# Gate logits of two batches in one PSUM bank: sharing the turn and the choice of experts

## The chip, the cores and the metric

The kernel runs on one core of one Trainium2 chip. The metric is the device time of one execution in microseconds (us). The kernel before takes 679.64 us, the median of three runs (679.59 to 681.14). The profile comes from one further execution, whose span is 676.8 us; positions in the trace count from its start.

The engines go by these names: PE is TensorE (matrix products), PEld is its loading of weights, DVE is VectorE, ACT is ScalarE, POOL is GpSimd and SP is SyncE, which here issues transfers. A step of the loop is one pass of the attention loop shown below, numbered by its `n`.

## The reference: what is computed

Attention with a local mask in half of the heads and a strided one in the others, followed by a mixture of experts in which a position may keep the expert of the position before it. Cut to what matters:

```python
# attention: batch 8, heads 8, positions 576, head size 64
scores = scale * np.matmul(q, k.transpose(0, 1, 3, 2))
scores = np.where(masks, scores, -1e9)          # local: rel < 32; strided: same residue mod 32
attn = softmax(scores)
x = np.matmul(attn, v)                          # -> x[b, s, 512]
...
# experts: E = 8, hidden size 1024
logits = np.einsum('bsd,de->bse', x, w_gate)    # 8 gate logits of a position
local_gate = sigmoid(x @ w_local)               # one more column
for b in range(B):
    for s in range(S):
        fresh_e = argmax(logits[b, s])
        e = fresh_e if s == 0 or local_gate[b, s] < 0.5 else prev_e
        prev_e = e
        p = softmax(logits[b, s])
        out[b, s] = p[e] * (relu(x[b, s] @ w1[e]) @ w2[e])
```

The nine columns (8 gates and the local gate) are one small matrix of weights, padded to 32 columns. All of it is float32.

## The kernel before: the parts concerned

Attention runs batch by batch, four pairs of heads to a batch. A step `n` of the loop starts the scores of pair `n`, multiplies the values of pair `n - 2` and transposes the result of pair `n - 3`, so that `x` of a batch lies turned (features on partitions) in `xT`. With the fourth pair of batch `b` turned, in step `n = 4b + 7`, the gate logits of that batch are made:

```python
wgs = consts.tile([P, DK, GC], F32, name="wgs")          # GC = 32 columns, 9 of them used
...
sel = consts.tile([P, E + 1], F32, name="sel")           # 1 where row % 32 == column
...
def gates(b):
    xT = st["xT", b]
    gl = rows.tile([P, S], F32, name="gl")
    for a in range(2):                                   # two halves of 288 positions
        s = slice(a * (S // 2), (a + 1) * (S // 2))
        pg = psX.tile([P, 512], F32, name="xps")         # one PSUM bank
        for kk in range(DK):                             # 4 parts of the 512 features
            pe(nc.tensor.matmul, pg[kk * GC:(kk + 1) * GC, 0:S // 2], lhsT=wgs[:, kk, :], rhs=xT[:, kk, s],
               start=True, stop=True)
        nc.scalar.copy(out=gl[:, s], in_=pg[:, 0:S // 2])
    st["gl", b] = gl
```

The four parts of the features land on four groups of 32 rows. Of each group the first nine rows hold something. The next function adds the four groups and turns the logits at once, by a product with `sel` (positions now on partitions, 6 blocks of 96), and chooses:

```python
def choices(b):
    gl = st["gl", b]
    ps = psX.tile([P, 512], F32, name="xps")
    for t in range(LT):                                  # 6 blocks of 96 positions
        pe(nc.tensor.matmul, ps[0:LQ, t * (E + 1):(t + 1) * (E + 1)], lhsT=gl[:, t * LQ:(t + 1) * LQ],
           rhs=sel, start=True, stop=True)
    lt = small.tile([LQ, LT, E + 1], F32, name="lt")
    nc.scalar.copy(out=lt, in_=...)
    nc.vector.tensor_reduce(mx, lg, axis=AX.X, op=Alu.max)
    nc.vector.tensor_tensor(ex, lg, mxb, op=Alu.subtract)
    nc.scalar.activation(ex, ex, Act.Exp)
    yield
    # next step: seven small operations of VectorE (eq, eq, code, code, fr, codes ...)
    nc.vector.tensor_tensor(codes[:, :, b], spread(code, [LQ, LT, E]), spread(fr, [LQ, LT, E]), op=Alu.mult)
    yield
    # the step after it: four more (sum, + 1e-9, reciprocal, product), then the gates are written out
    nc.sync.dma_start(out=xd[b * S:(b + 1) * S, D:DX]..., in_=ex)
    yield
```

The loop, in which the order of each engine's instructions is fixed as it is written:

```python
for n in range(len(pairs) + 6):
    if n < len(pairs):
        ...                                              # loads of a later batch (SyncE)
        for u in pairs[n]:
            scores(u)                                    # PE "sps", then ACT exp -> e
    last = pairs[n - 4][0] if 0 <= n - 4 < len(pairs) else None
    done = last.b if last and last.pair == PAIRS - 1 else None
    if done is not None:
        gates(done)
        ...
    for g in range(2):
        mask_out(pairs[n][g])                            # DVE, e * mask
        values(pairs[n - 2][g])                          # PE "vps", DVE reciprocal and product -> xl, xs
        if g == 0:
            next(chosen, None)
            if done is not None:
                chosen = choices(done)
                next(chosen)
    ...                                                  # store_x: POOL writes xl, xs out to xd
    turn_x(...)                                          # PE transposes "xps", ACT copies -> xT
```

Between these, pieces of `route` are placed: from step 17 on it routes the first three batches (BE = 3), from the `codes` of batches 0 to 2, on TensorE and VectorE; and pieces of the first expert's products fill the end of the stage. After attention `route` runs again for all eight batches beside the first experts.

Of the kernel before, what the change touches and what calls it, by code (L numbers as in the profile page):

```python
# [9 lines left out]
F32 = mybir.dt.float32  # L10
BF16 = mybir.dt.bfloat16
I32 = mybir.dt.int32
# [7 lines left out]
P = 128  # L20
# [63 lines left out]
def spread(ap, shape):  # L84

    dims = list("abcd"[:len(shape) - 1])
    left = " ".join(dims[:-1] + [f"({dims[-1]} o)"])
    right = " ".join(dims + ["o"])
    return ap.rearrange(f"{left} -> {right}", o=1).to_broadcast(shape)


def across(ap, shape):

    return ap.rearrange("a (o b) -> a o b", o=1).to_broadcast(shape)
# [177 lines left out]
def attention(ctx, tc, careful, psX, psS, fill, q, k, vl, vs, wg, xd, cc, codes, inv):  # L272
# [9 lines left out]
    small = ctx.enter_context(tc.tile_pool(name="small", bufs=3))  # L282
    psV = ctx.enter_context(tc.tile_pool(name="psV", bufs=1, space=PSUM))

    wgs = consts.tile([P, DK, GC], F32, name="wgs")


    maskL = consts.tile([LK, LQ], F32, name="maskL")
# [45 lines left out]
    nc.vector.tensor_scalar(ri, ri, GC - 1, None, Alu.bitwise_and)  # L334
    rf = consts.tile([P, 1], F32, name="rf")
    nc.vector.tensor_copy(rf, ri)
    ce = consts.tile([P, E + 1], I32, name="ce")
    nc.gpsimd.iota(ce, pattern=[[1, E + 1]], base=0, channel_multiplier=0)
    sel = consts.tile([P, E + 1], F32, name="sel")
    nc.vector.tensor_copy(sel, ce)  # L340
    nc.vector.tensor_scalar(sel, sel, rf, None, Alu.is_equal)

# [18 lines left out]
    def pe(product, *args, **kw):  # L361

        with tc.issue_after(st["pe"]) if "pe" in st else nullcontext():
            st["pe"] = product(*args, **kw).ins  # L364
# [19 lines left out]
    def load_first():  # L384


        for n in range(2 * PAIRS + 2):
            if n == PAIRS + 2:
                nc.sync.dma_start(out=wgs, in_=wg.rearrange("(k p) e -> p k e", p=P))
            if n < 2 * PAIRS:  # L390
                b, pair = divmod(n, PAIRS)
                grp, i2 = divmod(pair, 2)
                if i2 == 0:
                    places(b, grp)
                qt, kt = st["q", b, grp], st["k", b, grp]
                hq, hk = LT // 2 * LQ, LT // 2 * LQ + STRIDE
                for c, d in (((slice(0, hq), slice(0, hk)), (slice(hq, S), slice(hk, KW))) if n == 0 else
                             ((slice(0, S), slice(0, KW)),)):
                    nc.sync.dma_start(out=qt[:, i2, c], in_=q[b][:, pair, c])
                    (nc.sync if n else nc.scalar).dma_start(out=kt[:, i2, d], in_=k[b][:, pair, d])  # L400
            if n >= 2:
                b, pair = divmod(n - 2, PAIRS)
                grp, i2 = divmod(pair, 2)
                nc.sync.dma_start(out=st["v", b, grp][:, i2], in_=(vs if grp else vl)[b][:, i2])
# [90 lines left out]
    def turn_x(b, pair):  # L495
        grp, i2 = divmod(pair, 2)
        if pair == 0:
            st["xT", b] = rows.tile([P, DK, S], F32, name="xT")
        src = st["x", b, grp]
        o = st["xT", b][:, pair, :]  # L500
        o = (o.rearrange("x (i s p) -> x s i p", s=2, p=LQ // 2) if grp == 0 else
             o.rearrange("x (s p c) -> x s p c", s=2, c=STRIDE))
        for g in range(2):
            u = pairs[b * PAIRS + pair][g]
            r, m = u.rows, u.m
            ps = psX.tile([P, 512], F32, name="xps")
            for i in range(m):
                pe(nc.tensor.transpose, ps[:, i * P:i * P + r], src[0:r, u.t0 + i, i2 * P:(i2 + 1) * P],
                   ident[0:r, 0:r])
            if grp == 0:  # L510
                nc.scalar.copy(out=o[:, :, 3 * g:3 * g + 3].rearrange("x s i p -> x i s p"),
                               in_=ps[:, 0:m * P].rearrange("x (i s p) -> x i s p", i=m, s=2)[:, :, :, 0:LQ // 2])
            else:
                c, n = SBLK[u.t0]
                pt = ps[:, 0:m * P].rearrange("x (i s p) -> x s i p", i=m, s=2)[:, :, :, 0:n * SP // 2]
                for s in range(2):
                    nc.scalar.copy(out=o[:, s, :, c:c + m * n].rearrange("x p (i c) -> x i p c", i=m),
                                   in_=pt[:, s].rearrange("x i (p c) -> x i p c", c=n))

    def gates(b):  # L520

        xT = st["xT", b]
        gl = rows.tile([P, S], F32, name="gl")
        for a in range(2):
            s = slice(a * (S // 2), (a + 1) * (S // 2))
            pg = psX.tile([P, 512], F32, name="xps")
            for kk in range(DK):
                pe(nc.tensor.matmul, pg[kk * GC:(kk + 1) * GC, 0:S // 2], lhsT=wgs[:, kk, :], rhs=xT[:, kk, s],
                   start=True, stop=True)
            nc.scalar.copy(out=gl[:, s], in_=pg[:, 0:S // 2])  # L530
        st["gl", b] = gl

    def filling():
        with tc.issue_after(st["pe"]):
            st["pe"] = next(fill).ins

    def choices(b):

        gl = st["gl", b]
        ps = psX.tile([P, 512], F32, name="xps")  # L540
        for t in range(LT):
            pe(nc.tensor.matmul, ps[0:LQ, t * (E + 1):(t + 1) * (E + 1)], lhsT=gl[:, t * LQ:(t + 1) * LQ],
               rhs=sel, start=True, stop=True)
        lt = small.tile([LQ, LT, E + 1], F32, name="lt")
        nc.scalar.copy(out=lt, in_=ps[0:LQ, 0:LT * (E + 1)].rearrange("p (t e) -> p t e", e=E + 1))
        lg = lt[:, :, 0:E]
        mx = small.tile([LQ, LT], F32, name="gmx")
        nc.vector.tensor_reduce(mx, lg, axis=AX.X, op=Alu.max)
        mxb = spread(mx, [LQ, LT, E])
        ex = small.tile([LQ, LT, E], F32, name="ex")  # L550
        nc.vector.tensor_tensor(ex, lg, mxb, op=Alu.subtract)
        nc.scalar.activation(ex, ex, Act.Exp)
        yield

        eq = small.tile([LQ, LT, E], F32, name="eq")
        nc.vector.tensor_tensor(eq, lg, mxb, op=Alu.is_equal)
        nc.vector.tensor_tensor(eq, eq, across(down, [LQ, LT, E]), op=Alu.mult)
        code = small.tile([LQ, LT], F32, name="code")
        nc.vector.tensor_reduce(code, eq, axis=AX.X, op=Alu.max)
        nc.vector.tensor_tensor(code, pos8, code, op=Alu.subtract)  # L560
        fr = small.tile([LQ, LT], F32, name="fr")
        nc.vector.scalar_tensor_tensor(fr, lt[:, :, E], FRESH, start, Alu.is_le, Alu.max)

        nc.vector.tensor_tensor(codes[:, :, b], spread(code, [LQ, LT, E]), spread(fr, [LQ, LT, E]), op=Alu.mult)
        yield
        sm = small.tile([LQ, LT], F32, name="gsm")
        nc.vector.tensor_reduce(sm, ex, axis=AX.X, op=Alu.add)  # L567
        nc.vector.tensor_scalar(sm, sm, 1e-9, None, Alu.add)
        nc.vector.reciprocal(out=sm, in_=sm)
        nc.vector.tensor_tensor(ex, ex, spread(sm, [LQ, LT, E]), op=Alu.mult)  # L570
        nc.sync.dma_start(out=xd[b * S:(b + 1) * S, D:DX].rearrange("(t p) e -> p t e", p=LQ), in_=ex)
        yield

    pairs = [[Unit(b, pair, g) for g in range(2)] for b in range(B) for pair in range(PAIRS)]
# [7 lines left out]
    for n in range(len(pairs) + 6):  # L582
        if n < len(pairs):
            b, pair = divmod(n, PAIRS)
            if n >= PAIRS and pair % 2 == 0 and b + 1 < B:
                load(b + 1, pair // 2)
            for u in pairs[n]:
                (scores_shifted if careful else scores)(u)

        last = pairs[n - 4][0] if 0 <= n - 4 < len(pairs) else None  # L590
        done = last.b if last and last.pair == PAIRS - 1 else None
        if done is not None:
            gates(done)
            if done == B - 1:
                filling()
        yield n, 0, (st["pe"], st["dve"])
        for g in range(2):
            if n < len(pairs) and not careful:
                mask_out(pairs[n][g])
            if g == 0:  # L600
                yield n, 1, (st["pe"], st["dve"])
            if 0 <= n - 2 < len(pairs):
                values(pairs[n - 2][g])
            if g == 0:
                with tc.issue_after(st["dve"]):
                    next(chosen, None)
                    if done is not None:
                        chosen = choices(done)
                        next(chosen)
                if done == B - 1:  # L610
                    filling()
                yield n, 2, (st["pe"], st["dve"])
        if 0 <= n - 2 < len(pairs):
            u = pairs[n - 2][1]
            if u.i2 == 1:
                store_x(u.b, u.grp)
        if 0 <= n - 3 < len(pairs):
            u = pairs[n - 3][0]
            turn_x(u.b, u.pair)
            if n - 3 >= len(pairs) - 2:  # L620
                filling()
# [702 lines left out]
```

## Time and profile before

| what | value |
|---|---|
| time, median of three | 679.64 us (679.59 to 681.14) |
| span of the profiled execution | 676.8 us |
| first matmul of the scores | 7.66 us |
| last turning of gates starts (batch 7) | 145.15 us |
| gate matmuls, mean | 128, 412 ns |
| turning matmuls, mean | 96, 231 ns |
| copies of gates PSUM to SBUF (ACT) | 16, 399 ns |
| copies of turned logits (ACT) | 8, 200 ns |
| granted TensorE clock | 0.99 |

The busy time of an engine is the sum of its instructions' spans. Matmuls overlap, so the mean of one is longer than the distance to the next. A matmul of float32 shows as two instructions, each with a weight load of its own. In the profile's lines a group is written as line, engine, operation, output `<-` inputs, shapes, count, then busy time and mean, and then the engine's idle time just before the group with what ended it. Products, masks and normalisations that a helper issues all have the helper's line (L364 for TensorE, L369 for VectorE) and are told apart by their tiles: `sps` scores, `vps` values, `xps` transposes, gates and turning. The chain of waits follows the work that ended last back to what released each piece.

### The profile page before, as it was taken

To read this page: it belongs to the slowest core of one execution; us is meant where nothing else is said; L and a number is where in the kernel's file an instruction comes from. 1 tells how busy PE (TensorE), PEld (TensorE's weight loads), DVE (VectorE), ACT (ScalarE), POOL (GpSimd) and SP (SyncE) were. 2 spreads that over 40 slices of the span, in tenths; PEclk is the share of its full clock that TensorE was granted. 3 is DMA by queue.
4 is the path that set the end of the run, shared out by engine and by line. 5 is a ranking of instruction groups with operands and counts; after the bars stand their busy time and mean duration, and the time that the engine had idled before them with its cause. 6 is when DMAs were issued, how large, how long until landed. Compare 5 with 4: busy or idle time off the path is not lost.

```text
span 676.8 us, 14748 instructions
## 1 busy us (share of the span) xinstructions
PE 653.5 (97%) x5962; PEld 555.9 (82%) x5962; DVE 395.8 (58%) x840; ACT 191.4 (28%) x402; POOL 165.0 (24%) x200
## 2 busy tenths in 40 slices
PE   8999999999999999999999999999999999999980
PEld 7888888877767799996699984999999996869970
DVE  8677899734562556855285664468568540205660
ACT  4555555521111131231133121322313311113220
POOL 2444343740035214201221402112112011011210
PEclk9999999999999999999999999999999999999995
DMA  9999999559989978775867857674687759577200
GB/s 324 404 406 408 297 311 350 175 143 396 399 291 327 386 281 303 284 280 200 307 218 287 296 207 284 212 245 158 238 302 262 280 177 322 210 262 299 64 17 21
DMA packets 70850, 179.95 MB, mean 266 GB/s; under 512 B 12110, under 2 KB 12622, under 8 KB 70768
## 3 DMA queue, kind: packets, MB, share of 16 engines
q1 hardware_dynamic: 58704, 148.47, 60.6%
q0 software_dynamic: 11776, 30.08, 13.2%
q8 instruction: 51, 0.84, 0.5%
q10 hardware_dynamic: 288, 0.31, 0.1%
q14 instruction: 31, 0.25, 0.1%
HBM read 159.80 MB, written 19.55 MB: 265 GB/s over the span
## 4 chain that ended last, share of the span: by engine, by line
PE 90%; DMA 4%; DVE 2%; issue 1%; POOL 0%; ACT 0%; SPq 0%; POOLq 0%; DVEq 0%
PE bank L1028 49%; PE bank L1177 10%; PE bank L1151 10%; PE vps L364 6%; PE sps L364 5%; PE xps L364 5%; PE bank L1173 2%; DMA w2t<-in_w_dram 2%; DMA xd<-xs 2%; PE sps L1151 1%; DMA kt<-in_k_dram 1%; DVE w2t L1010 0%; DVE t L1012 0%; DVE t L1011 0%; PE bank L836 0%
## 5 line engine op out<-in xcount | busy, mean ns | idle before, releaser
L1187 POOL DMA_INDIRECT out_dram<-y,si x38 | 50.6, 1331 | 274.3 <-DVE y L1096 139.8
L971 POOL DMA_INDIRECT xg<-xd,gi x42 | 55.2, 1315 | 141.9 <-PE bank L1028 127.2
L1177 PE MATMUL bank<-w2t,hT 128*128 128x512 f32 x160 | 70.7, 594 | 0.8 <-ACT hT L1154 0.8
L1151 PEld LDWEIGHTS bank<-xgT,w1t 128*128 128x128 f32 x576 | 65.4, 192 | 2.0 <-issue 1.7
L1151 PE MATMUL bank<-xgT,w1t 128*128 128x128 f32 x576 | 66.2, 276 | 0.0
L1177 PEld LDWEIGHTS bank<-w2t,hT 128*128 128x128 f32 x160 | 29.6, 190 | 34.1 <-issue 33.0
L493 POOL DMA_DIRECT2D xd<-xs x80 | 44.8, 568 | 46.4 <-DVE gsm L567 27.9
L1063 DVE TENSOR_TENSOR part<-bank,part 128x512 f32<-128x512 f32 x13 | 9.0, 691 | 78.7 <-ACT part L1060 78.7
L1028 PEld LDWEIGHTS bank<-xT,w1t 128*128 128x128 f32 x416 | 49.5, 192 | 3.1 <-issue 2.6
L1028 PE MATMUL bank<-xT,w1t 128*128 128x128 f32 x416 | 51.3, 276 | 0.0
L1028 PE MATMUL bank<-xs,w1t 128*128 128x128 f32 x416 | 50.7, 275 | 0.0
L1028 PE MATMUL bank<-xs,t 128*128 128x128 f32 x416 | 50.7, 275 | 0.0
L1028 PE MATMUL bank<-w2t,h 128*128 128x256 f32 x208 | 49.2, 379 | 0.0
L1028 PE MATMUL bank<-t,hs 128*128 128x256 f32 x208 | 49.1, 379 | 0.0
L1028 PE MATMUL bank<-w2t,hs 128*128 128x256 f32 x208 | 49.1, 379 | 0.0
L1028 PEld LDWEIGHTS bank<-xs,w1t 128*128 128x128 f32 x416 | 48.5, 192 | 0.0
L1028 PEld LDWEIGHTS bank<-xs,t 128*128 128x128 f32 x416 | 48.5, 192 | 0.0
L1053 DVE TENSOR_TENSOR h<-bank,part 128x512 f32<-128x512 f32 x39 | 26.9, 691 | 34.7 <-ACT part L1065 22.9
L364 PE MATMUL sps<-qt,kt 64*128 64x96 f32 (+2 forms) x704 | 45.8, 275 | 1.1 <-DMA kt<-in_k_dram 1.0
L364 PEld LDWEIGHTS sps<-qt,kt 64*128 64x128 f32 (+2 forms) x704 | 40.2, 183 | 5.9 <-issue 2.3
L1093 ACT ACTIVATE part<-bank,pt 128x256 f32<-128x256 f32 x39 | 18.5, 473 | 92.0 <-PE bank L1028 92.0
L1028 PEld LDWEIGHTS bank<-w2t,hs 128*128 128x128 f32 x208 | 39.6, 190 | 5.3
(270 smaller groups left out, 1054.5 us busy)
## 6 DMA issues: line engine op xcount, KB each, us to landing
w1t<-in_w_dram SPq DMA_DIRECT2D x56, 1024.0 KB, 7.4
w2t<-in_w_dram SPq DMA_DIRECT2D x56, 1024.0 KB, 7.2
kt<-in_k_dram SPq DMA_DIRECT2D x12, 608.0 KB, 8.8
qt<-in_q_dram SPq DMA_DIRECT2D x12, 576.0 KB, 7.9
vlt<-in_vl_dram SPq DMA_DIRECT2D x6, 780.0 KB, 9.0
xd<-xl POOLq DMA_DIRECT2D x16, 288.0 KB, 6.8
vst<-in_vs_dram SPq DMA_DIRECT2D x6, 650.0 KB, 9.0
xd<-xs POOLq DMA_DIRECT2D x48, 54.0 KB, 5.8
```

The source lines that it names most:

```text
L364: st["pe"] = product(*args, **kw).ins
L493: nc.gpsimd.dma_start(out=dst[h, :, c:c + n], in_=src[h * HALF:h * HALF + n * SP // 2, t])
L971: self.nc.gpsimd.indirect_dma_start(out=u["xg"][:, a] if "pair" in u else u["xg"], out_offset=None, in_=self.xd[0:u["rows"]], in_offset=ba ...
L1028: self.end = fn(*args, **kw).ins
L1053: nc.vector.tensor_tensor(to, ps, add, op=Alu.add)
L1063: nc.vector.tensor_tensor(u, b7, u, op=Alu.add)
L1093: nc.scalar.activation(to, ps, Act.Copy, scale=g[r])
L1151: ins = nc.tensor.matmul(ps[:, i * P:(i + 1) * P], lhsT=w1[:, kk, c], rhs=xT[:, kk * P:(kk + 1) * P], start=(kk == 0), stop=(kk == DK - 1))
L1173: ins = nc.tensor.matmul(ps[s], lhsT=hT[:, kk, s], rhs=w[:, kk, :], start=(kk == 0), stop=(kk == FK - 1))
L1177: ins = nc.tensor.matmul(ps, lhsT=hT[:, kk], rhs=w2[:, kk, :], start=(kk == 0), stop=(kk == FK - 1))
L1187: self.nc.gpsimd.indirect_dma_start(out=self.views[0], in_=y, in_offset=None, bounds_check=N - 1, oob_is_err=False, out_offset=bass.Indire ...
```

## The change

In the kernel before, each batch's nine rows of logits leave 23 of each 32 rows of the bank empty, and the turning and choosing are done once a batch. The change puts a second batch into rows 16 to 24 of each group. The weights stand in a wider tile, with 16 columns of zeros ahead. The first batch of a pair uses columns 16 to 47, so that its logits land on rows 0 to 8 of a group. The second uses columns 0 to 31, so that its logits land on rows 16 to 24, and it is added to the first in the same bank. One set of turning products with an 18-column `sel` then gives both batches' logits, and one set of small operations chooses for both. Batch 0 and batch 7 stay by themselves; batches 1 and 2, 3 and 4, 5 and 6 are taken together, at the time at which the second one is done. Two batches' `xT` must be held for that, so `xT` gets two buffers.

```diff
-    wgs = consts.tile([P, DK, GC], F32, name="wgs")
+    wgs = consts.tile([P, DK, GC + GC // 2], F32, name="wgs")
+    nc.vector.memset(wgs[:, :, 0:GC // 2], 0.0)
 ...
-    ce = consts.tile([P, E + 1], I32, name="ce")
-    nc.gpsimd.iota(ce, pattern=[[1, E + 1]], base=0, channel_multiplier=0)
-    sel = consts.tile([P, E + 1], F32, name="sel")
+    ce = consts.tile([P, 2 * (E + 1)], I32, name="ce")
+    nc.gpsimd.iota(ce, pattern=[[GC // 2, 2], [1, E + 1]], base=0, channel_multiplier=0)
+    sel = consts.tile([P, 2 * (E + 1)], F32, name="sel")
 ...
-            st["xT", b] = rows.tile([P, DK, S], F32, name="xT")
+            st["xT", b] = rows.tile([P, DK, S], F32, name="xT", bufs=2)
 ...
-    def gates(b):
+    def gates(bs):
 ...
-            for kk in range(DK):
-                pe(nc.tensor.matmul, pg[kk * GC:(kk + 1) * GC, 0:S // 2], lhsT=wgs[:, kk, :], rhs=xT[:, kk, s],
-                   start=True, stop=True)
+            for i, b in enumerate(bs):
+                w = wgs[:, :, GC // 2:] if i == 0 else wgs[:, :, 0:GC]
+                for kk in range(DK):
+                    pe(nc.tensor.matmul, pg[kk * GC:(kk + 1) * GC, 0:S // 2], lhsT=w[:, kk],
+                       rhs=st["xT", b][:, kk, s], start=(i == 0), stop=(i == len(bs) - 1), skip_group_check=True)
 ...
-    def choices(b):
+    def choices(bs):
 ...
         for t in range(LT):
-            pe(nc.tensor.matmul, ps[0:LQ, t * (E + 1):(t + 1) * (E + 1)], lhsT=gl[:, t * LQ:(t + 1) * LQ],
-               rhs=sel, start=True, stop=True)
+            pe(nc.tensor.matmul, ps[0:LQ, t * w:(t + 1) * w], lhsT=gl[:, t * LQ:(t + 1) * LQ], rhs=sel[:, 0:w],
+               start=True, stop=True)
 ...  # the small tiles become [LQ, LT, n, ...] with n = len(bs), and bufs=2 for 3
-        nc.vector.tensor_tensor(codes[:, :, b], spread(code, [LQ, LT, E]), spread(fr, [LQ, LT, E]), op=Alu.mult)
+        nc.vector.tensor_tensor(codes[:, :, bs[0]:bs[-1] + 1], spread(code, wide), spread(fr, wide), op=Alu.mult)
 ...
-        nc.sync.dma_start(out=xd[b * S:(b + 1) * S, D:DX].rearrange("(t p) e -> p t e", p=LQ), in_=ex)
+        for i, b in enumerate(bs):
+            nc.sync.dma_start(out=xd[b * S:(b + 1) * S, D:DX].rearrange("(t p) e -> p t e", p=LQ), in_=ex[:, :, i])
 ...
         done = last.b if last and last.pair == PAIRS - 1 else None
+        done = None if done is None else [done] if done in (0, B - 1) else [done - 1, done] if done % 2 == 0 else None
```

## The prediction

> **What bounds the kernel now.** I read first the busy line of the page, and then the list of what TensorE waited for over the whole span.
>
> ```profile
> PE 653.5 (97%) x5962; PEld 555.9 (82%) x5962; DVE 395.8 (58%) x840; ACT 191.4 (28%) x402; POOL 165.0 (24%) x200
> ```
>
> ```profile
> engine line waited for: us in total, times, longest us
> PE xps L364 <- POOL ident masks.py:199: 1.5, 1, 1.5
> PE sps L364 <- DMA kt<-in_k_dram: 1.0, 1, 1.0
> PE bank L1173 <- DVE hT L1133: 0.9, 2, 0.6
> PE bank L1177 <- ACT hT L1154: 0.8, 1, 0.8
> PE xps L641 <- DVE codes L564: 0.3, 1, 0.3
> ```
>
> 97% alone proves nothing, since matmuls overlap and a busy TensorE need not be a full one. The second view decides: between the first keys (7.66 us) and the end of the attention stage (about 148 us) TensorE waits once, for 0.3 us, until the first three batches' codes are made. TensorE works through its list there without a gap, so what leaves the list should shorten the run.
>
> How long each piece takes I read in the chain of waits between 37 and 53 us, where the chain is TensorE alone (start, length, what, number of matmuls).
>
> ```profile
> ...
> 39.05 1.21 PE sps L364 x20
> 40.26 1.50 PE vps L364 x48
> 41.76 0.68 PE xps L364 x5
> 42.44 1.21 PE sps L364 x20
> 43.64 1.11 PE xps L364 x16
> 44.75 0.82 PE vps L364 x24
> 45.57 1.12 PE xps L364 x12
> 46.69 0.82 PE vps L364 x24
> 47.50 0.72 PE xps L364 x6
> ...
> ```
>
> Three lines are a plain step of the loop (10): scores, values, transposes. Six are step 11, which also ends batch 1: 16 gate matmuls (1.11), and 12 matmuls that turn the gates (1.12), put between the two halves of the values. The parts hold for other batches too, which the busy table of these stretches shows. Its rows are step 10, step 11, step 15 (batch 2), step 19 (batch 3) and step 27 (batch 5); columns are length, then the busy time of each engine.
>
> ```profile
> 38.98:42.37 3.39, 3.39 (x75) 3.02 (x74) 2.97 (x10) 2.15 (x7) 3.32 (x7) 1.00 1.02 413
> 42.37:48.16 5.79, 5.79 (x104) 4.67 (x103) 3.83 (x11) 2.97 (x10) 2.28 (x5) 1.00 1.03 403
> 58.53:64.32 5.79, 5.79 (x103) 4.66 (x102) 3.82 (x11) 2.97 (x10) 2.41 (x5) 1.00 1.05 392
> 76.26:82.05 5.79, 5.79 (x104) 4.66 (x103) 4.73 (x12) 2.97 (x10) 1.67 (x3) 1.00 0.87 249
> 110.76:116.56 5.80, 5.80 (x104) 4.67 (x103) 5.55 (x15) 2.98 (x10) 2.29 (x5) 1.00 1.06 368
> ```
>
> A step that ends a batch is 5.79 us whatever the batch, and a plain one with the same scores 3.39. VectorE has two spare microseconds in step 11 (3.83 of 5.79) and next to none in step 27 (5.55 of 5.80), where routing the first three batches runs beside the attention. That matters below.
>
> The groups by form over the first 150 us give the operations that the change touches.
>
> ```profile
> L364 PE MATMUL xps<-xT,wgs 128*32 128x288 f32 x128 | 9.4, 412 | 0.0
> L364 PE MATMUL xps<-sel,gl 128*96 128x9 f32 x96 | 9.4, 231 | 0.0
> L364 PEld LDWEIGHTS xps<-sel,gl 128*96 128x96 f32 x96 | 8.8, 165 | 0.6
> L557 DVE TENSOR_TENSOR eq<-eq,down 96x48 f32<-96x48 f32 x8 | 1.6, 196 | 0.0
> ```
>
> Per batch that is 16 gate matmuls and 12 turning ones, twice what the code writes: each float32 matmul appears as two instructions.
>
> **What the Trainium skill says.** TensorE: Matmul & The Clock Gate, section LDWEIGHTS, says that a weight load's time goes with its columns and not with its rows. The trace agrees in kind: loads of 32, 48, 96 and 128 columns average 109, 123, 165 and 192 ns. The turning matmuls load 96 columns of gates to move only 9. They are 93 ns apart (1.12 us over 12), which is the price of loading; twice the moved columns is nearly free. TensorEngine Tiling (Array Packing), section Key Properties, says that changing the tiling mode drains TensorE. Values cut in two by the turning take 0.82 + 0.82 us, uncut 1.50, so 0.14 us goes with each removed turning, and I put it down to that. VectorE: DVE Perf Modes, section The TRN2 errata, gives a float32 add as (N + 151) cycles at 0.96 GHz; 48 elements would be an estimated 207 ns, the trace has 196. By the same formula another 48 elements cost an estimated 50 ns.
>
> **The change part by part.** Batches 1 and 2, 3 and 4, 5 and 6 become pairs; 0 and 7 stay alone. gates(b) runs in step 4b + 7, so the work of batches 1, 3 and 5 (steps 11, 19, 27) moves to the steps of their partners (15, 23, 31).
>
> Steps 11, 19 and 27 become plain. A plain local step is 3.39 us when five transposes end it; theirs has six, 0.72 instead of 0.68 us, so 3.43. Each saves 5.79 - 3.43 = 2.36 us.
>
> Steps 15, 23 and 31 get 16 more gate matmuls. These come four column groups at a time; at 77.46 us the first four start within 0.27 us, so 16 more take 1.08 us. They add up where they used to overwrite zero, but number and shapes stay. The turning keeps its 12 instructions with 18 moved columns for 9. In the 512-column matmuls of the experts 12 take 5.35 us, 0.87 ns a column, so the nine extra columns cost at most 8 ns each, 0.1 us in all. Together +1.18 us.
>
> Net for TensorE: 2.36 - 1.18 = 1.18 us a pair, 3.54 us for three.
>
> ScalarE loses two 0.40 us copies of gates, one 0.20 us copy of logits and one 0.25 us exponential per pair, and the remaining two grow slightly. It is busy about half the stage and nothing on TensorE's list waits longer for it: this lies beside other work. VectorE loses 11 small operations per pair. They overlap, so each occupies about 0.12 to 0.15 us, and some 1.5 us goes per pair; the 11 that stay grow, seven of them by up to 50 ns, so 0.3 us returns. The second xT buffer lets two batches wait at once; with one buffer the gates already stood ahead of the next batch's first transposes. The memset (64 columns once), the table with 18 columns and two small writes of gates per pair are off the path: keys, not VectorE, hold the first matmul.
>
> What returns is where TensorE runs up against VectorE.
> - Step 17 waits for the codes of batch 2, 0.31 us today. Four or five wider operations lie in that chain, at 50 ns: 0.2 us more, once.
> - In steps 19 to 21 TensorE comes 2.36 us earlier, but VectorE only by its idle waits there (0.44 + 0.55 us) plus the gone maximum and difference (0.25), some 1.25 us. The second half of the values in step 20 starts at about 84.2 us and needs a buffer whose normalisation ends at 83.24. Shifted, that is 81.85 against 82.0. A similar margin in step 21 makes about 0.35 us of waiting in all.
> - In steps 27 and 28 VectorE builds the routing table: the product with it starts at 118.07 us, and its last piece of lanes ends at 116.61. Moved 2.36 and about 0.4 us earlier, they stand at 115.7 and 116.2: a wait of about 0.55 us, after which VectorE has caught up.
>
> Sum: 3.54 - 0.2 - 0.35 - 0.55 = 2.44 us, on 679.64 us: 677.2. Steps 23 and 31 give VectorE more time than now, so part of the waits may vanish; I take 677.1. After the attention stage nothing is touched and the rest should only move forward.
>
> **The rivals.** First: TensorE's saving passes whole, 3.54 us, 676.1. For it: in the list of waits VectorE never stops TensorE for longer than 0.3 us in this stage. Against it: 5.55 of 5.80 us busy in step 27.
>
> Second: VectorE becomes the bound of the routing steps, and the two pairs (3, 4) and (5, 6) bring next to nothing: 1.18 - 0.2 = 1 us, 678.6. For it: VectorE busy 7.79 of 8 us between 88 and 96. Against it: the change takes its operations away too, and its longest gaps are in the very steps that lengthen.
>
> Third: a transfer. The chain passes from 54 to 67 us through stores of x (DMA xd<-xs, 5.75 and 5.13 us), and the 16 DMA engines stand at 1.03 of their time until 64 us. If VectorE had to wait for those stores, the 2.36 us of step 11 would be lost: about 678. I don't believe it: before each such write to xs stand four semaphore instructions of 50 ns, and a gap of 0.2 us appears also at 102.4 and 134.6 us, where no store is named. And xs has two buffers, so the store that counts is one batch older.
>
> Fourth: 16 accumulating gate matmuls onto one bank instead of 8 delay the gates' copies, and the turning waits for ScalarE. Today the second copy ends at 61.38 and turning starts at 61.66. As the first copy now falls beside the second bank's matmuls, the margin should hold; if not, 0.3 us a pair is lost, 678.
>
> **Range and chances.** The best case, all of TensorE's gain and a little draining less, is about 676; the second or third rival with small losses ends near 679. I take 675.9 to 679.0 for 8 in 10. A 2% change is 13.6 us, four times all that the change moves on TensorE, so within 2% is nearly certain.
>
> **What would show it.** Right: steps 11, 19 and 27 without gates, 3.4 us if VectorE doesn't hold them; steps 15, 23 and 31 near 6.9 us; 60 turning matmuls still near 93 ns apart, 128 gate matmuls as before; the attention stage some 2.4 us shorter and everything later only shifted. Short new waits of TensorE's loads for VectorE would appear in steps 20, 21 and 28, and the wait for codes would be near 0.5 us. Wrong: the turning taking visibly more than 1.2 us, gates above 2.3 us, TensorE waiting for a store or for ScalarE, or a new stall in the experts' stage.

## The result, and the profile after

| | before | after |
|---|---|---|
| time, median | 679.94 us (679.59 to 681.14, 4 runs) | 676.92 us (676.49 to 677.92, 4 runs) |
| span of the profiled execution | 676.8 us | 674.9 us |
| step 11 / 15 / 17 | 5.79 / 5.79 / 4.43 us | 3.43 / 6.77 / 4.63 us |
| step 19 / 20 / 21 / 22 / 23 | 5.79 / 3.52 / 3.65 / 3.52 / 5.79 | 3.44 / 3.53 / 3.77 / 3.74 / 6.96 |
| step 27 / 28 / 29 | 5.80 / 4.06 / 3.47 | 3.65 / 4.38 / 4.27 |
| scores of step 6 to the first output product | 126.87 us | 125.17 us |

The ratio is 0.9955, with a 95% interval of 0.9937 to 0.9972: 3.0 us at the medians, and 1.9 to 4.3 us by the interval. 677.1 was predicted. The times alone cannot tell 2.4 us from 3.5, so the traces have to. The length of a step is the distance from its first scores to those of the next. The last row is a ruler that I use below. It runs from the start of the scores of step 6 to the start of the first product with `w2t`, and so leaves out both ends of the kernel: in the fourteen traces of this document the scores of step 6 start at 21.8 to 23.2 us, and what follows the first output product takes 527.1 to 531.0 us. Step 7, whose work is the same in every kernel here, takes 5.79 us in some traces and 6.07 in others, the first of before among them; these 0.28 us are in the ruler, and I name them where they matter.

The busy line of the page after the change, and the list of what TensorE waited for:

```profile
PE 652.1 (97%) x5926; PEld 554.1 (82%) x5926; DVE 392.7 (58%) x805; ACT 188.7 (28%) x390; POOL 156.3 (23%) x200
```

```profile
engine line waited for: us in total, times, longest us
...
PE xps L652 <- DVE codes L572: 0.5, 1, 0.5
...
PE vps L366 <- issue: 0.4, 1, 0.4
PE vps L366 <- DVE xl L371: 0.3, 1, 0.3
```

TensorE has lost 36 instructions, the 12 turning matmuls of three batches. VectorE has lost 35: choosing takes 12 operations (six and not seven of them in the step of the codes), so 36 are gone, and the memset is one more. The wait for codes has gone from 0.3 to 0.5 us. Two short waits of the values are new. The one put down to "issue", which is time in which the profile shows nothing that was waited for, stands in step 29. The one for VectorE's `xl` stands at 132.34 us, in step 32; the waits for `xl` in steps 27 and 28, which are discussed next, leave TensorE idle by 0.1 us and less, and show in the length of the steps instead.

The chain of waits over steps 11 and 15 (start, length, what, number of matmuls) shows the shared turning at work:

```profile
42.26 1.21 PE sps L366 x20
43.46 1.50 PE vps L366 x48
44.97 0.72 PE xps L366 x6
...
56.06 1.21 PE sps L366 x20
57.26 2.08 PE xps L366 x32
59.34 0.82 PE vps L366 x24
60.16 1.12 PE xps L366 x12
61.28 0.82 PE vps L366 x24
62.10 0.73 PE xps L366 x6
```

Step 11 is now plain, with its values in one piece. Step 15 has 32 gate matmuls in 2.08 us and still 12 turning ones in 1.12 us. Per instruction, in the groups by form over the first 150 us:

```profile
L366 PE MATMUL xps<-xT,wgs 128*32 128x288 f32 x128 | 8.8, 410 | 0.0
L366 PE MATMUL xps<-sel,gl 128*96 128x18 f32 x36 | 3.7, 238 | 0.1
L366 PE MATMUL xps<-sel,gl 128*96 128x9 f32 x24 | 2.3, 228 | 0.0
L564 DVE TENSOR_TENSOR eq<-eq,down 96x96 f32<-96x96 f32 x3 | 0.7, 240 | 0.0
```

Busy time counts spans that overlap once, so 128 spans of 410 ns are 8.8 us. All 128 gate matmuls are still there; 96 turning matmuls have become 60; twice the columns cost a turning matmul 10 ns of its span and nothing of its spacing. Choosing has 60 operations of VectorE where it had 96, and a wide one such as this is 44 ns longer (196 ns before, 240 now).

The busy table of steps 11 and 15 (length, then busy time of PE, PEld, DVE, ACT, POOL) shows TensorE full in both:

```profile
42.26:45.69 3.43, 3.43 (x76) 3.09 (x76) 2.86 (x7) 2.10 (x7) 1.63 (x3) 1.00 1.03 407
56.06:62.83 6.77, 6.77 (x120) 5.18 (x120) 3.73 (x11) 3.14 (x10) 2.37 (x5) 1.00 1.03 409
```

Where time is lost late in the stage is seen in steps 28 and 29, again in the chain of waits:

```profile
112.99 0.93 DVE lane L841 x2
113.92 0.59 DVE e L371
114.65 0.57 DVE xl L371
115.26 0.68 PE vps L366 x16
...
118.18 1.25 PE vps L366 x32
119.43 0.38 issue
119.80 0.47 PE vps L366 x8
```

The first three lines are VectorE catching up: lanes of the routing table, a mask, a normalisation, and only then can TensorE go on with the values. The 0.38 us of "issue" in step 29 are something else, a pause in the middle of a run of values. In the first trace of the kernel before, step 29 has none. Steps 22 and 23 hold such pauses too, 0.23 and 0.19 us: without them they are 3.51 and 6.77 us long, as in several runs below.

### The profile page after: what moved, and what is told of

Its sections match the earlier page's. It is cut to its first block, busy times and chain, and to the rows that moved or that the text cites. A ratio compares the mean times of both kernels' runs of the same rounds, so it can differ in the third digit from the quotient of the medians.

```text
span 674.9 us, 14639 instructions
## 1 busy us (share of the span) xinstructions
PE 652.1 (97%) x5926; PEld 554.1 (82%) x5926; DVE 392.7 (58%) x805; ACT 188.7 (28%) x390; POOL 156.3 (23%) x200
## 4 chain that ended last, share of the span: by engine, by line
PE 90%; DVE 4%; DMA 2%; issue 1%; ACT 0%; POOL 0%; DVEq 0%; POOLq 0%; ACTq 0%
PE bank L1039 49%; PE bank L1188 10%; PE bank L1162 10%; PE vps L366 6%; PE xps L366 5%; PE sps L366 5%; PE bank L1184 2%; DMA w2t<-in_w_dram 2%; PE sps L1162 1%; DVE e L371 1%; DVE xl L371 0%; DVE lane L841 0%; DVE xs L371 0%; DVE t L1023 0%; DVE w2t L1021 0%
## 5 line engine op out<-in xcount | busy, mean ns | idle before, releaser
L982 POOL DMA_INDIRECT xg<-xd,gi x42 | 47.5, 1131 | 146.3 <-PE bank L1039 128.6
L423 ACT ACTIVATE e<-sps 128x576 f32<-128x576 f32 (+1 forms) x64 | 39.9, 649 | 15.7 <-PE sps L366 12.4
```

The costliest lines, as they stand in the source:

```text
L423: nc.scalar.activation(ev, ps[0:kb, :, 0:m * w], Act.Exp, bias=0.0, scale=1.0 / DH ** 0.5)
L982: self.nc.gpsimd.indirect_dma_start(out=u["xg"][:, a] if "pair" in u else u["xg"], out_offset=None, in_=self.xd[0:u["rows"]], in_offset=ba ...
```

## The experiments

My theory: TensorE's list sets the end of the stage; the gain is the removed turnings, and what is lost of it is lost where VectorE is behind. Rivals: merely moving work later does it; the sharing of VectorE's small operations does it; the pauses are caused by the change.

**The changed kernel again, unchanged.**

> The changed kernel once more, unaltered, for a narrower interval and a second trace. Theory (TensorE's list decides, and three sets of 12 turning matmuls are gone): about 2.5 to 3 us below the kernel before, ratio near 0.996. The plain steps 11, 19 and 27 save 2.36 us each and steps 15, 23 and 31 cost about 1 us each, as in the first trace. If the delays of TensorE in step 29 (+0.8 us) and in steps 31 and 32 (+0.6 us) of the first trace belong to the kernel's order of work they come again at the same places; if they were an accident of that execution the attention stage is up to 1.4 us shorter this time.

677.55 us (676.94 to 678.18, 7 runs), ratio 0.9951 (0.9933 to 0.9968). Its steps lie within 0.1 us of those above: 3.43, 6.77, 4.64, 3.71 (step 22), 6.95, 3.64, 4.39, 4.18. The delays of step 29 and of steps 31 and 32 came again at the same places. The ruler gives 125.14.

**Late, but not shared.** Each batch keeps its own gates, turning and choice, but both of a pair are done at the later step.

```diff
-            for i, b in enumerate(bs):
-                w = wgs[:, :, GC // 2:] if i == 0 else wgs[:, :, 0:GC]
+        for b in bs:                       # a bank and a gl of its own for each batch
+            ... lhsT=wgs[:, kk, GC // 2:], rhs=st["xT", b][:, kk, s], start=True, stop=True
-                        chosen = choices(done)
+                        chosen = zip(*[choices([b]) for b in done])
```

> The gates of batches 1, 3 and 5 move to the step of their partner, as in the change, but each batch keeps its own bank, its own turning and its own choice: only the time of the work changes, not its amount. Theory (the shared turning is what saves): TensorE's list is as long as before, so 679.9 us, within 1 us of the kernel before; steps 11, 19, 27 lose 2.36 us and steps 15, 23, 31 gain 2.3 to 2.4 us. Rival (fewer interruptions and a calmer order save): about 677, like the change.

685.12 us, where 679.9 was expected, ratio 1.0068 (1.0044 to 1.0092). Steps 11 and 19 are 3.43, steps 15 and 23 are 8.02: what leaves one step enters the other (2.36 out, 2.23 in). That part came as expected. The ruler is 130.05 us, though, 3.2 above the first trace of before. VectorE being behind costs 0.69 us in step 27 (4.12 instead of 3.43), 0.32 in step 28 (4.38), and 0.69 in step 33, where two whole choices meet the last steps. The chain of waits there:

```profile
137.40 0.56 DVE xs L371
...
138.96 0.24 DVE codes L571 x2
...
140.25 0.68 PE vps L366 x16
```

Two more losses have no name in the trace: 0.82 us of pauses in step 29 (4.29), and 1.5 us in steps 31 and 32, where the chain is TensorE alone but slower than elsewhere (six transposes in 1.31 us instead of 0.72). The time is longer by more than that, 4.7 us against the kernel before in the same set of runs; its six runs have granted clocks of 0.979 to 0.986, where the kernel before has 0.987 to 0.990, so part of it may go with the clock. Being late is not free: the last steps have no scores of their own behind which VectorE's work could lie. Moving alone is no part of the gain, then; it is a cost that the sharing has to earn first.

**Gates and turning shared, small operations apart.** VectorE's operations and the exponential are done once for each batch again.

```diff
+        for i in range(n):
+            lg, m, x = lt[:, :, i, 0:E], mx[:, :, i], ex[:, :, i]
+            nc.vector.tensor_reduce(m, lg, ...); nc.vector.tensor_tensor(x, lg, ...); nc.scalar.activation(x, x, Act.Exp)
 ...                                       # the other ten operations likewise
```

> Gates and turning of two batches are shared as in the change, but the small operations of VectorE and the exponential are done for each batch by itself, so VectorE has as many small operations as before. Theory (TensorE's list decides): the list is that of the changed kernel, and only the wait for the codes in step 17 grows, from 0.5 to about 1.1 us: about 677.5 us, at most 1 us above the changed kernel. Rival (the operations taken off VectorE and ScalarE save): back at 679 to 680 us.

678.60 us, ratio 0.9965 (0.9952 to 0.9979); ruler 126.32, so 3.73 us come off the late kernel. In step 15 it is 1.25 us: 1.02 for the second turning, and 0.24 because 32 gate matmuls in banks of their own take 2.32 us instead of 2.08. In step 23 a pause in this trace (0.64 us idle) leaves 0.52 of it, and from step 31 on it is 2.03, because the late kernel lost more there; that the sum is near three times 1.25 is luck. From here to the full change it is 1.15 us more: 0.47 in step 27 (4.12 to 3.65), 0.64 in step 33, where the choices of batches 5 and 6 stand beside the last values, and 0.54 in step 23, which is the pause; steps 17 and 22 go the other way by 0.55 and 0.13, and 0.17 lies in steps 31 and 32. So the relief of VectorE gives some 1.1 us where VectorE is behind, a smaller part than the turning. Timed side by side the two kernels are 1.05 us apart. Against the expectation the wait for codes in step 17 didn't grow but vanished (4.08 us). The last experiments come back to that.

**Turning twice, in the kernel before.** Batches 1, 3 and 5 are turned a second time into unused columns of the same bank, which nothing reads.

```diff
+        if b in (1, 3, 5):
+            for t in range(LT):
+                pe(nc.tensor.matmul, ps[0:LQ, 256 + t * (E + 1):256 + (t + 1) * (E + 1)],
+                   lhsT=gl[:, t * LQ:(t + 1) * LQ], rhs=sel, start=True, stop=True)
```

> The kernel before, in which batches 1, 3 and 5 turn their gates twice, the second time into unused columns of the same bank: 36 matmuls more, each 93 ns apart. Theory (TensorE's list decides in this stage): 3 x 1.12 = 3.4 us longer than the kernel before, 683.3 us. Rival (TensorE has hidden slack there, and the change gained elsewhere): less than 1 us longer.

The chain of waits of step 11:

```profile
45.12 0.82 PE vps L364 x24
45.94 2.14 PE xps L364 x24
48.07 0.82 PE vps L364 x24
```

24 matmuls take 2.14 us where 12 took 1.12: the second set costs 1.02 us, and each of steps 11, 19 and 27 grew by just that, to 6.81. The price of a turning is settled: 1.02 for the matmuls and 0.14 for cutting the values, and all of it shows in the step. The time, 688.49 us (ratio 1.0113, 1.0086 to 1.014), is more than the 3.1 us of this (the ruler, 130.98 us, is 2.6 above that of the run in the next experiment). Its single runs go from 685.22 us at a granted clock of 0.987 to 690.76 at 0.978, and 0.009 of 685 us is 6 us; so most of the excess goes with the clock. What lowered it isn't shown.

**The kernel before again, unchanged.**

> The kernel before once more, for a second trace of it: how far do the start (first keys), the steps and what comes after the last instruction move from one execution to another? Expected: steps within 0.1 us of the first trace; start and end up to 1 to 2 us apart, as the traces of the altered kernels differ there.

All steps are those of before within 0.02 us, but step 29 is 4.95 us instead of 3.47. The chain of waits of this run shows why:

```profile
121.71 0.94 PE vps L364 x20
122.65 0.40 issue
123.04 0.35 PE vps L364 x3
123.39 0.38 issue
```

These are the same pauses as after the change, in the same step, so those of step 29 don't belong to the change. The ruler of this run is 128.35, 1.48 above the first trace's. Against it the changed kernel is 3.18 us shorter; the first pair of traces alone would have said 1.7. Neither is the change by itself: the changed kernel's trace holds 1.86 us of pauses and delays (0.23, 0.19, 0.80 and 0.64 us in steps 22, 23, 29 and from 31 on), and both traces of before hold the 0.28 us of step 7.

**Without the choice of rows, after and before.** GpSimd's gathers of the chosen rows for the first experts become plain copies of the first rows of `x`. This leaves out the choice of rows, and the experts compute on other rows; the amount of work is the same.

```diff
+        if j < NE:
+            self.nc.gpsimd.dma_start(out=u["xg"], in_=self.xd[j * P:(j + 1) * P])
+            return
         for a, i in enumerate(u["cols"]):
             self.nc.gpsimd.indirect_dma_start(...)
```

> The changed kernel, but the first six tiles of rows for the experts are read as plain rows in order, not gathered by the routing table: it leaves out the choice of rows for the first experts, so its output is not the reference's, while every engine's work in the attention stage stays. GpSimd has no gathers by index in steps 29 to 31. Theory (the delays of TensorE in step 29, +0.8 us, and of VectorE and TensorE in steps 31 and 32, +0.6 us, come from gathers that run at that moment): both vanish, step 29 is 3.5 us and the first output product starts about 1.4 us earlier counted from step 6. Rival (they come from VectorE's backlog or from TensorE itself): steps 29 to 32 stay as long as in the changed kernel.

> The kernel before, with the first six tiles read as plain rows as in e6, so that neither side has gathers by index in the attention stage: it leaves out the choice of rows for the first experts. Theory (the pauses of TensorE in steps 29 to 32 come with those gathers and belong to neither kernel alone): step 29 is 3.5 us, the first output product starts 126.9 us after step 6, and e6_plain_rows (123.3) is 3.1 to 3.6 us below it, which is the change by itself: three times 2.36 - 0.98 saved, less 0.2 (codes), 0.35 (steps 20 to 22) and 0.53 (steps 27 and 28) of waits for VectorE. Rival (the change is worth only the 1.7 us that the first two traces differ by): this kernel starts its first output product near 125 us after step 6.

Neither has a pause: step 29 is 3.47 us in both, and steps 22 and 23 of the changed kernel are 3.51 and 6.77. The ruler gives 123.31 and 126.60 us, so 3.29 us for the change with the pauses out of the way, and the steps account for all of it: 2.36 each in steps 11 and 19 and 2.15 in step 27, less 0.98 each in steps 15 and 23 and from 31 on, and less 0.20, 0.11 and 0.32 in steps 17, 21 and 28. By pairs that is 1.2 us for (1, 2), 1.3 for (3, 4) and 0.85 for (5, 6). Timed, the kernels take 675.75 (ratio 0.9923, 0.9903 to 0.9943) and 678.96 us (1.0000, 0.9991 to 1.0008), 3.21 us apart. The two ratios differ by more, 5 us, but the kernel before that each is measured against takes 681.12 us in one set of runs and 679.35 in the other. Against these the plain copies gain the changed kernel something and the kernel before nothing, so what the pauses cost on average is left open. Steps 27 and 28 keep their 3.64 and 4.38 us: those waits are the change's own. Step 22 loses its excess, so that one was not.

**Two mask products of steps 26 and 27 on GpSimd.** If VectorE's backlog makes the waits of steps 27 and 28, taking two products (0.67 us each) off it there should remove them.

```diff
+        if u.n in (53, 55):
+            nc.gpsimd.tensor_tensor(blocks(ev, m), blocks(ev, m), mask, op=Alu.mult)
+        else:
             dve(nc.vector.tensor_tensor, blocks(ev, m), blocks(ev, m), mask, op=Alu.mult)
```

> The changed kernel, in which GpSimd and not VectorE multiplies the second mask of steps 26 and 27 (0.67 us of VectorE each). Theory (VectorE's backlog from the routing table holds TensorE in steps 27 and 28, by 0.21 and 0.33 us): both waits go, step 27 is 3.43 and step 28 4.06 us, about 0.5 us in all. Rival (something other than VectorE's load holds those steps): they stay 3.65 and 4.38 us.

Step 27 is 3.43 us, the plain length: that wait was VectorE's backlog. The expectation failed for step 28, however. Step 28 is 5.87 instead of 4.38, and the time 679.63 us (ratio 0.9975, 0.9962 to 0.9988). The uses of `lane` in this run (count, then shortest, median and longest time in ns), GpSimd's two products (start, length), and the longest wait of TensorE:

```profile
L844 DVE TENSOR_TENSOR lane<-io,lo x6: 544/546/2867, 109.7 to 114.1; 96x384 bf16<-96x384 f32 x6
```

```profile
114.26 2.30 POOL L431 TENSOR_TENSOR e<-e,maskS 126x504 f32<-126x504 f32 x2
```

```profile
PE xps L850 <- DVE lane L844: 1.6, 1, 1.6
```

One `lane` operation takes 2.87 us instead of 0.55, in just the time in which GpSimd works on its products (114.26 to 116.56; both run in step 28 only, so the one of step 26 comes late), and TensorE's product with the table waits 1.6 us for it. The Trainium skill, SBUF — State Buffer, section "Who interferes with whom", says that a VectorE instruction with two SBUF inputs contends with a GpSimd instruction that reads SBUF. The trace agrees, and the price here is 2.3 us.

**Only two pairs.** Batches 5 and 6 are taken alone again, with the choice of rows and without it.

```diff
-[done] if done in (0, B - 1) else [done - 1, done] if done % 2 == 0 else None
+{0: [0], 2: [1, 2], 4: [3, 4]}.get(done, [done] if done > 4 else None)
```

> The changed kernel with only the pairs (1, 2) and (3, 4); batches 5, 6 and 7 go alone as before. By the steps of the two traces pair (1, 2) brings 1.2 us, pair (3, 4) 0.8 us, and pair (5, 6) costs 0.6 us, because its work comes into steps 31 to 33, which have no scores to hide VectorE's and ScalarE's part. Theory: the first output product starts some 2 us earlier than in the kernel before, counted from step 6, 0.3 to 0.6 us better than the changed kernel. Rival (each turning saved is worth 1.2 us wherever it is): 1 us worse than the changed kernel.

> Pairs (1, 2) and (3, 4) only, as in e8, with plain rows as in e6. Against e6_plain_rows it tells what the pair (5, 6) is worth when no gather disturbs. Theory: 1.38 us of TensorE less 0.53 us of waits in steps 27 and 28, so the first output product starts 0.8 to 0.9 us later than in e6, near 124.2 us after step 6. Rival (pair (5, 6) costs time because its choice falls into the last steps): it starts earlier than in e6, before 123.3 us.

With the choice of rows: 678.64 us (0.9969, 0.9957 to 0.9981) and 126.44 on the ruler, 1.27 more than with three pairs; but steps 22, 23 and 29 hold 1.04 us more of pauses here, and steps 31 and 32 hold 0.64 us less. Without the choice: 676.66 us (0.9960, 0.9946 to 0.9975), 0.91 more than with three pairs, and 124.45, 1.14 more, of which 0.27 is step 7. What is left in steps 27, 28 and from 31 on is some 0.86 us in both comparisons, as the second expectation had it. I had held the third pair to be a loss, because I believed the one undisturbed trace of before; it is worth nearly 0.9 us.

**Codes ahead of the mask.** VectorE's order explains the step 17 of the run with apart choices. Here is VectorE in step 17 of the changed kernel (start, length):

```profile
66.09 0.24 DVE L563 TENSOR_TENSOR eq<-lt,gmx 96x96 f32<-96x96 f32 x1
...
66.33 0.74 DVE L371 TENSOR_TENSOR e<-e,maskL 128x576 f32<-128x576 f32 x1
...
67.97 0.25 DVE L572 TENSOR_TENSOR codes<-code,fr 96x96 f32<-96x96 f32 x1
```

A mask product of 0.74 us, and a product of `x` after it, stand between the first comparison and the codes for which TensorE waits. They stood there in the kernel before too; in the two runs with twice as many narrow operations, late only and apart choices, all of these had come ahead of them. One line fixes that order, for batches 1 and 2 alone, or for all pairs:

```diff
-        nc.vector.tensor_tensor(codes[:, :, bs[0]:bs[-1] + 1], ...)
+        made = nc.vector.tensor_tensor(codes[:, :, bs[0]:bs[-1] + 1], ...)
+        if bs[0] == 1:                     # all pairs: if len(bs) == 2
+            st["dve"] = made.ins           # the next mask product is issued behind it
```

> The changed kernel, but for batches 1 and 2 VectorE's order is fixed so that their codes come ahead of the next mask product (0.75 us) in step 17; in the changed kernel that product and a 0.33 us product of x stand between the first comparison and the codes. Theory (TensorE's 0.5 us wait for codes is set by that order and not by the width of the operations, as the run with apart choices suggested with a step 17 of 4.08 us): step 17 is 4.1 us instead of 4.63, the wait for codes is gone, steps 18 to 20 stay at 3.99, 3.44 and 3.53, and the first output product comes 0.4 to 0.6 us earlier than in the changed kernel; time 676.4 where the changed kernel would take 676.9. Rival (the mask product is late now and TensorE waits for the masked scores one step later instead): steps 18 and 19 together grow by 0.3 to 0.5 us, time 676.9.

> As the run before it, for all three pairs: codes ahead of the mask product in steps 17, 25 and 33. Theory (VectorE is behind in steps 25 to 28 whatever the order within a step): step 17 as in the run before it, step 25 and the steps behind it within 0.1 us of the run before it, time the same within 0.5 us. Rival (masked scores come too late in step 25, where VectorE has no time to spare): steps 25 to 28 together grow by 0.4 to 1 us.

For batches 1 and 2 alone, VectorE's list becomes:

```profile
66.03 0.24 DVE L563 TENSOR_TENSOR eq<-lt,gmx 96x96 f32<-96x96 f32 x1
...
67.08 0.26 DVE L572 TENSOR_TENSOR codes<-code,fr 96x96 f32<-96x96 f32 x1
67.25 0.74 DVE L371 TENSOR_TENSOR e<-e,maskL 128x576 f32<-128x576 f32 x1
```

The codes start 1.05 us after the first comparison instead of 1.88, step 17 is 4.08 us, the wait for codes is gone from TensorE's list, and steps 18 to 20 stay at 3.98, 3.43 and 3.54. 675.84 us (674.35 to 676.3, 6 runs), ratio 0.9941 (0.9923 to 0.996): the fastest of the kernels here that leave nothing out, though its interval overlaps that of the change. The ruler says 123.41, 1.76 below the changed kernel, more than the 0.4 to 0.6 expected: 0.55 from step 17, 0.23, 0.80 and 0.64 from step 22, step 29 and steps 31 and 32, which have no pause in this trace, less 0.20 for a longer one in step 23 and 0.28 for step 7. Step 22 has its 3.51 us also in runs that leave the order alone. So 0.55 us can be put down to the order, as expected, and the rest is the pauses' luck.

For all pairs it is 676.84 us (0.9959, 0.9944 to 0.9973). Step 25 is the same to 0.01 us; step 27 grows from 3.64 to 3.90, and values wait for VectorE late in the stage:

```profile
PE vps L366 <- DVE xs L371: 0.4, 1, 0.4
```

The ruler is 123.95, 0.54 above the other: 0.26 from step 27 and 0.67 from step 33, where this wait stands, less the 0.39 us of pause that the other run has in step 23. The rival was right in kind here, smaller in the steps that it named and with a larger loss in one that it did not name: where VectorE is behind, choosing first holds up what TensorE needs next, and routing needs the codes only of the first three batches.

## Why the prediction was right, step by step

| term of the sum | predicted | measured |
|---|---|---|
| steps 11, 19, 27 become plain, each | -2.36 | -2.36, -2.35; step 27 counted below |
| second set of gates, each | +1.08 | +0.98 (2.08 against 1.11) |
| turning with 18 columns, each | at most +0.10 | 0.00 (1.12 and 1.12) |
| wait for codes, step 17 | +0.20 | +0.20 |
| VectorE late, steps 19 to 21 | +0.35 | +0.12, nearly all in step 21 |
| VectorE late, steps 27 and 28 | +0.55 | +0.53 (0.21 and 0.32) |
| sum | -2.44 | -3.29 |

The measured sum takes step 27 as 2.36 less 0.21. It is three times 1.38, less 0.85, and is what the ruler gives for the two kernels without the choice of rows. The timed 3.0 us agrees within its interval.

**What held.** TensorE's list set the end of the stage, and a removed turning came back in full. What was lost of the gain was lost mostly where TensorE ran up against VectorE.

**Sizes that were off.** "Together +1.18 us" was 0.98. I had priced the second set of gates from four starts within 0.27 us, and the set runs a little closer; and I charged nine more columns at the rate of 512-column matmuls. The Trainium skill, TensorE: Matmul & The Clock Gate, section LDWEIGHTS, which the prediction used, says that a load's time goes with its columns, and these stay 96; the trace agrees, 1.12 us for 12 matmuls either way. Three times 0.20 is 0.6 us. The wait in steps 19 to 21 was put at three times its size, which is 0.23 us more: the margin in step 20 held (3.54 us against 3.52), and step 21 lost 0.11. Step 22, which is longer by 0.23 us in the first trace after the change, had a pause and no wait for VectorE. Together these are the 0.85 us by which the sum was too small. The time came nearer to the forecast than the sum did; part of that is luck. VectorE loses 12 operations per pair, not 11, which changes nothing here.

**A right number with a wrong cause.** The step that failed is "Moved 2.36 and about 0.4 us earlier, they stand at 115.7 and 116.2: a wait of about 0.55 us". TensorE's product with the table did not wait: its 18 matmuls start from 113.73 to 114.17 us without a gap, and the last lanes were done at 113.92, before their turn came. VectorE was behind with the normalisation instead, so that the second half of the values waited, in steps 27 and 28, as the chain shows for step 28. So the match of 0.55 with 0.53 is luck. With VectorE relieved of two mask products the wait of step 27 went. For step 28 that run shows nothing, since it put a larger wait there.

**A wait that I took as given.** I raised the 0.31 us for codes by 0.2 for width. That was right as a sum, and the run with codes first shows that the whole 0.5 us hung on VectorE's order.

**What I had not foreseen.** The pauses, 0.80 us in step 29 against the first trace of before, and 1.86 us with the delays of steps 22, 23, 31 and 32. A single trace of before was a poor ruler; a second one has 1.48 us of them in step 29.

**The rivals.** The first, all of 3.54, was closest in time but not in mechanism: there are 0.85 us of losses, and larger savings (4.14 us). It lies nearer to the 3.29 us than my own sum does. The second, VectorE as the bound that leaves pairs (3, 4) and (5, 6) with nothing, fell: they bring some 1.3 and 0.85 us. The third, stores, fell: the gap of 0.2 us ahead of the writes to `xs` is 0.2 us still, with step 11 2.36 us shorter. The fourth, ScalarE's copies of the gates, fell: no wait for them stands in TensorE's list.

## What to carry to other kernels

Where small matmuls are paid for their weights, put more columns behind one load, and count the cuts that they make in other work as well. Work that is shared later must also be affordable later: the same shift without sharing lost time, because it met an engine that was already behind. Before taking a wait for another engine as given, read the order of that engine's list: here one mask product among six small operations was worth half a microsecond. A second trace of the unchanged kernel was worth more than a finer reading of the first, and a comparison is safe when its steps, one by one, add up to the whole.

## What the hardware showed beside this

**TensorE probably waits for its own instructions.** In step 23 TensorE pauses in six of the ten traces of kernels with pairs, always behind the second of the 12 turning matmuls, and the step grows by 0.2 to 1.0 us. With apart choices the chain of waits has:

```profile
92.61 0.27 PE xps L366 x2
92.89 0.64 issue
93.53 0.94 PE xps L366 x10
```

In all six the third matmul starts 2.2 to 2.4 us after a 16 KB transfer has begun on the DMA queue q8, which the page calls "instruction". In the four traces without the pause that transfer begins 2.8 to 4.2 us ahead of the same matmul. The short pause of step 22, in four traces, ends 2.3 to 2.4 us after the start of the transfer before that one. What makes these transfers late isn't shown, and no run tests it. The four traces of kernels without pairs have no pause in these steps, so these pauses, unlike those of step 29, may belong to the change.

**Pauses without a name.** In step 29 TensorE pauses once to three times, for 0.34 to 0.40 us each, with nothing named. Step 29 has this in eight of eleven traces with GpSimd's gathers (not in the first of before, nor in the two with codes first), and in none of the three without gathers. That hints at the gathers but doesn't settle it. VectorE pauses too: in step 31 of the changed kernel it starts its first reciprocal after 3.18 us of idle time, and with codes first after 1.77; TensorE is 0.64 us longer in steps 31 and 32. Both causes stay open.

**Two engines in each other's way.** A VectorE product over two SBUF inputs went from 0.55 to 2.87 us beside a GpSimd product.

**Twelve more cost less than the first twelve.** Twelve more turning matmuls directly behind twelve others took 1.02 us (85 ns each) against 1.12 for the first twelve, and 32 gate matmuls took 2.08 us against twice 1.11.
